# Linear-attention kv blocks: sixteen 128-column matmuls replaced by pairs on 64-column tiles, placed ahead of the normalizer's batch

## The chip, the cores and the metric

The kernel runs on one core of one Trainium2 chip. The metric is the device time of one execution in microseconds (us), lower is better. Each run lists the span and clock of one core alone, so there is no other to compare with, and a run counts as fast when it is within 1.5% of the fastest of its kernel.

## The reference

Two branches are mixed by a gate. Only branch A matters here: linear attention with 32 heads of 16 columns.

```python
qkv = (x @ wqkv)...            # x: (1, 2048, 512); H = 32 heads of Dh = 16
pq, pk = phi(q), phi(k)        # phi(t) = where(t > 0, t + 1, exp(t)) + 1e-6
kv  = einsum("bhsd,bhse->bhde", pk, v)     # one 16 x 16 block per head
z   = einsum("bhsd->bhd", pk)
num = einsum("bhqd,bhde->bhqe", pq, kv)
den = einsum("bhqd,bhd->bhq", pq, z) + 1e-6
a   = (num / den) @ wo
# ... branch B: layer norm, two matmuls over the sequence (w1, w2) with a gelu between
out = g * a + (1 - g) * b
```

## The kernel before

The kernel never forms v. It accumulates gT = (pk transposed times x) transposed, and gets the kv blocks from gT and the weights wv. Only the 16 x 16 blocks on the diagonal are wanted, so the product is taken for four diagonal blocks of 128 x 128 and multiplied with a mask. The masked blocks times wo give W2, which is used by the output tiles.

```python
    def kv_matmuls():                              # ND = 4, P = 128
        kvps = bank("kvps")                        # 128 x 512 f32
        for j in range(ND):
            for k in range(ND):
                mm(
                    kvps[:, j * P : (j + 1) * P], wv_sb[:, k, j * P : (j + 1) * P],
                    gT[:, k, j * P : (j + 1) * P], k == 0, k == ND - 1,
                )
        nc.vector.tensor_tensor(
            out=kvbdT[:], in0=kvps[:].rearrange("p (j d) -> p j d", j=ND),
            in1=mask[:].unsqueeze(1).to_broadcast([P, ND, P]), op=ALU.mult,
        )

    def den_matmuls():                             # the normalizer: already on four 32-column tiles
        denps = bank("denps")
        for j in range(ND):
            for c in range(NSC):                   # NSC = 4
                mm(
                    denps[32 * c : 32 * c + 32, :], Z32[:, 32 * j : 32 * j + 32], pqT[:, j, c * SC : (c + 1) * SC],
                    j == 0, j == ND - 1, tile_position=(0, 32 * c),
                )
        ...  # rden = reciprocal(denps) on VectorE

    for t in range(NT):                            # the q-projection stage, NT = 16
        for jj in range(NB0):
            mm(accs[jj][:], w1c[0][:, t, jj * P : (jj + 1) * P], hs[:, t, :], t == 0, t == NT - 1)
        q_block(t)
        ...
        if t == 4:
            kv_matmuls()
        ...
    for j in range(NB0, NF):                       # the w1 blocks, sixteen matmuls each
        ...  # acc += w1 block j times hs; gelu(j, acc)
        if j == NB0 + 2:
            z_matmuls()
        if j == NB0 + 3:
            den_matmuls()
            gate_sums()
            ...
        if NB0 + 4 <= j < NB0 + 4 + ND:
            w2_matmul(j - NB0 - 4)                 # W2 = masked kv blocks times wo
    ...  # the output tiles: aps (A branch) and yps (B branch), 16 of them
```

## Time and profile before

| | before |
|---|---|
| time, median of 3 runs | 165.60 us (165.58 to 165.94) |
| span of the profiled execution | 163.6 us |
| tensor engine busy | 159.9 us, 98% |
| chain of waits | 98% tensor engine |
| kv batch on the chain | 0.89 us |

The first view is the page: the busy time of each engine with its share of the span and its number of instructions, and the chain of waits by engine.

```profile
PE 159.9 (98%) x785; PEld 73.6 (45%) x785; DVE 87.8 (54%) x200; ACT 58.7 (36%) x90; POOL 18.3 (11%) x37
...
PE 98%; DVE 0%; issue 0%
```

The chain is 98% tensor engine, so every nanosecond of its stream counts, and nothing else does as long as it stays hidden. The second view is the same chain in order of time. Its columns are the start in us, the length in us, what ran and how many of it.

```profile
40.07 0.86 PE qacc L108 x4
40.93 0.89 PE kvps L108 x16
41.82 0.65 PE uacc L108 x3
...
68.99 3.47 PE uacc L108 x16
72.46 0.98 PE denps L108 x16
73.44 3.56 PE uacc L108 x16
```

The kv batch is 0.89 us, sixteen steps of 56 ns. A 512-column matmul takes a step of 216 ns, so sixteen of them take 3.45 us; the normalizer's sixteen take only 0.98 us, because four tiles work at once (their starts lie within 10 ns, below). The block behind it takes 3.56 instead of 3.45 us. The timeline shows why. Its columns are start, length, engine, line, operation, output and inputs, sizes, count, and in brackets the idle time before it. PE is a matmul and PEld a weight load. A recorded matmul is longer than its step (379 ns on the page for 512 columns, against 216 ns from start to start), so the records overlap, and steps are read from starts.

```profile
40.55 1.09 PEld L108 LDWEIGHTS <-wv_sb 128*128 128x128 bf16 x16
40.77 1.06 PE L108 MATMUL kvps<-gT,wv_sb 128*128 128x128 bf16 x16
41.61 0.37 PEld L108 LDWEIGHTS <-w1c 128*128 128x128 bf16 x3
41.66 0.81 PE L108 MATMUL uacc<-hs,w1c 128*128 128x512 bf16 x3
...
72.39 0.55 PEld L108 LDWEIGHTS <-Z 128*32 128x32 bf16 x16 [0.42 <-issue]
72.39 1.05 PE L108 MATMUL denps<-pqT,Z 128*32 128x512 bf16 x16
...
73.36 3.14 PEld L108 LDWEIGHTS <-w1c 128*128 128x128 bf16 x16 [0.42 <-issue]
73.37 3.63 PE L108 MATMUL uacc<-hs,w1c 128*128 128x512 bf16 x16
```

Around the kv batch the weight loads run ahead of the matmuls (40.55 against 40.77 us) without a pause. Around the normalizer they pause, "0.42 <-issue", both when the 32-column tiles begin and when the full array returns. In the trace's records the last full matmul starts at 72.079 us and the first normalizer matmul at 72.388, 309 ns later, and the last normalizer matmul starts at 73.056 and the next full one at 73.368, 312 ns later. The step would be 216 ns in both places, so by these starts a change of tiling costs 93 to 96 ns. The sixteen normalizer matmuls start in four groups, the four tiles of a group within 10 ns.

### The profile page before, as it was taken

How to read it: one execution, taken by the hardware profiler on the slowest of the kernel's cores; microseconds unless marked ns; L12 is line 12 of the kernel's file. 1: busy time of each engine (PE TensorE's matmuls, PEld its weight loads, DVE VectorE, ACT ScalarE, POOL GpSimd, SP SyncE). 2: the span in 40 equal slices, each digit the busy share in tenths (PEclk: the TensorE clock that was granted, in tenths of full speed). 3: DMA queues.
4: the chain of work that ended last, by engine and by line, in shares of the span. 5: the costliest groups of instructions: out<-in, count | busy, mean ns of one | idle time of the engine just before them, and what ended most of it. 6: DMA issues, size and time to landing. Idle time of an engine off the chain costs nothing.

```text
span 163.6 us, 2078 instructions
## 1 busy us (share of the span) xinstructions
PE 159.9 (98%) x785; PEld 73.6 (45%) x785; DVE 87.8 (54%) x200; ACT 58.7 (36%) x90; POOL 18.3 (11%) x37
## 2 busy tenths in 40 slices
PE   7999999999999999999999999999999999999993
PEld 3444444444544444434444444444444444444452
DVE  0599999958999999109995301156221111111112
ACT  3463386658478373311332113111112222211110
POOL 5000710200200000001055500050000000000000
DMA  5999999999930005800993499932010000111001
GB/s 152 242 243 236 294 300 344 349 348 348 317 78 0 0 0 188 264 0 0 277 303 109 149 289 307 337 126 98 32 36 32 32 32 32 42 50 41 32 32 32
DMA packets 30057, 25.05 MB, mean 153 GB/s; under 512 B 7968, under 2 KB 29472, under 8 KB 30048
## 3 DMA queue, kind: packets, MB, share of 16 engines
q1 hardware_dynamic: 28032, 22.02, 45.5%
q0 software_dynamic: 1440, 2.38, 5.4%
q10 hardware_dynamic: 576, 0.52, 1.1%
q8 instruction: 6, 0.10, 0.2%
q14 instruction: 3, 0.02, 0.0%
HBM read 21.11 MB, written 2.23 MB: 143 GB/s over the span
## 4 chain that ended last, share of the span: by engine, by line
PE 98%; DVE 0%; issue 0%
PE uacc L108 30%; PE yps L108 30%; PE kacc L108 9%; PE aps L108 8%; PE qacc L108 8%; PE gacc L108 8%; PE wps L108 2%; PE pt L194 1%; PE denps L108 1%; PE kvps L108 1%; DVE ot L474 0%; PE zps L108 0%; PE pt L323 0%
## 5 line engine op out<-in xcount | busy, mean ns | idle before, releaser
L108 PE MATMUL uacc<-hs,w1c 128*128 128x512 bf16 x224 | 52.1, 379 | 0.0
L108 PE MATMUL yps<-uT,w2c 128*128 128x512 bf16 (+2 forms) x238 | 51.0, 366 | 0.0
L474 DVE SCALAR_TENSOR_TENSOR ot<-yps,c,a_sc 128x512 bf16<-128x512 f32 (+2 forms) x17 | 12.2, 720 | 45.9 <-PE yps L108 45.8
L108 PEld LDWEIGHTS <-w2c 128*128 128x128 bf16 x238 | 22.8, 98 | 25.9
L108 PEld LDWEIGHTS <-w1c 128*128 128x128 bf16 x224 | 21.7, 98 | 26.0 <-issue 0.4
L461 ACT ACTIVATE a_sc<-aps,c,gg 128x512 f32<-128x512 f32 x16 | 12.4, 778 | 46.7 <-PE aps L108 43.0
L317 ACT ACTIVATE uT<-uacc,bcol 128x512 bf16<-128x512 f32 x14 | 9.3, 687 | 27.7 <-PE uacc L108 27.7
L108 PE MATMUL aps<-W2sb,pqT 128*128 128x512 bf16 x64 | 16.4, 379 | 0.0
L108 PE MATMUL qacc<-xT,wq_sb 128*128 128x512 bf16 x64 | 16.4, 379 | 0.0
L108 PE MATMUL kacc<-wk_sb,xT 128*128 128x512 bf16 x64 | 16.4, 385 | 0.0
L108 PE MATMUL gacc<-pk,xs 128*128 128x512 bf16 x64 | 15.8, 379 | 0.0
L244 ACT ACTIVATE hs<-xs,nmr,rstd 128x512 bf16<-128x512 bf16 x16 | 12.8, 805 | 1.9 <-DVE nmr L238 1.9
L204 ACT ACTIVATE e<-qacc 128x512 bf16<-128x512 f32 x16 | 9.6, 597 | 10.1 <-PE qacc L108 9.2
L413 POOL DMA_DIRECT2D rex<-rd_dram x16 | 9.5, 603 | 23.0 <-DVE pqT L415 18.2
L204 ACT ACTIVATE e<-kacc 128x512 bf16<-128x512 f32 x16 | 9.3, 595 | 6.9 <-PE kacc L108 6.8
L208 DVE SCALAR_TENSOR_TENSOR pk<-kacc,e 128x512 bf16<-128x512 f32 x16 | 11.1, 692 | 0.6
L208 DVE SCALAR_TENSOR_TENSOR pqT<-qacc,e 128x512 bf16<-128x512 f32 x16 | 11.1, 692 | 0.6
L228 DVE BATCH_NORM_STATS2 stats<-xs 128x6 f32<-128x512 bf16 x16 | 10.9, 682 | 0.0
L205 DVE TENSOR_SCALAR e<-e 128x512 bf16<-128x512 bf16 x32 | 9.0, 282 | 3.3 <-ACT e L204 3.3
L400 DVE CUSTOM_DVE_ANT_0 junk<-xs,gw_b 128x512 bf16<-128x512 bf16 x16 | 9.8, 685 | 0.0
L269 DVE TENSOR_TENSOR zacc<-zacc,pk 128x512 f32<-128x512 f32 x14 | 9.6, 686 | 0.2
L108 PEld LDWEIGHTS <-wq_sb 128*128 128x128 bf16 x64 | 6.3, 98 | 7.5
(64 smaller groups left out, 70.1 us busy)
## 6 DMA issues: line engine op xcount, KB each, us to landing
w2c<-in_B_w_dram SPq DMA_DIRECT2D x8, 896.0 KB, 7.5
w1c<-in_B_w_dram SPq DMA_DIRECT2D x2, 2048.0 KB, 15.5
w1c<-in_B_w_dram SPq DMA_DIRECT2D x3, 1024.0 KB, 12.3
rex<-rd_dram POOLq DMA_DIRECT2D x16, 128.0 KB, 2.9
out_dram<-ot SPq DMA_DIRECT2D x15, 128.0 KB, 1.7
xs<-in_A_x_dram SPq DMA_DIRECT2D x3, 512.0 KB, 4.5
wq_sb<-in_A_wqkv_dram SPq DMA_DIRECT2D x1, 512.0 KB, 6.8
wv_sb<-in_A_wqkv_dram SPq DMA_DIRECT2D x1, 512.0 KB, 12.3
```

The costliest lines, as they stand in the source:

```text
L108: nc.tensor.matmul(o, lhsT=lhsT, rhs=rhs, start=start, stop=stop, **kw)
L204: nc.scalar.activation(out=e[:], in_=acc[:], func=ACT.Exp)
L205: nc.vector.tensor_scalar(out=e[:], in0=e[:], scalar1=1.0, scalar2=PHI_EPS, op0=ALU.min, op1=ALU.add)
L208: nc.vector.scalar_tensor_tensor(out=dst, in0=acc[:], scalar=0.0, in1=e[:], op0=ALU.max, op1=ALU.add)
L228: nc.vector.bn_stats(out=stats[:], in_=xs[:, t, :])
L244: nc.scalar.activation(out=hs[:, t, :], in_=xs[:, t, :], func=ACT.Identity, scale=rstd[:, t : t + 1], bias=nmr[:, t : t + 1],)
L269: nc.vector.tensor_tensor(out=zacc[:], in0=first, in1=pk[:, t, :], op=ALU.add)
L317: nc.scalar.activation(out=uT[:, j, :], in_=acc[:], func=ACT.Gelu_apprx_tanh, bias=bcol[:, j : j + 1])
L400: nc.vector.tensor_tensor_reduce(out=junk[:], in0=xs[:, t, :], in1=gw_b[:], scale=1.0, scalar=0.0, op0=ALU.mult, op1=ALU.add, accum_out=gp ...
L413: nc.gpsimd.dma_start(out=rex[:], in_=src.unsqueeze(1).to_broadcast([8, HEAD, SC]))
L461: nc.scalar.activation(out=a_sc[:], in_=aps[:], func=ACT.Identity, scale=gg[:, t : t + 1], bias=c2[:, t : t + 1],)
L474: nc.vector.scalar_tensor_tensor(out=ot[:, :W], in0=yps[:, :W], scalar=c1[:, t : t + 1], in1=a_sc[:, cs], op0=ALU.mult, op1=ALU.add,)
```

## The change

The intent is to compute only the two 64 x 64 diagonal blocks of each 128 x 128 block, on two 64-column tiles of the array that are to work side by side, as the normalizer's four do (starts within 10 ns), and to put them where the array is in a column-tiled mode anyway. The masking becomes two half-size operations, the untouched half of kvbdT is cleared once at the start, and the W2 products come one w1 block later.

```diff
+    nc.vector.memset(kvbdT[:], 0.0)
...
+    H2 = P // 2
     def kv_matmuls():
         kvps = bank("kvps")
         for j in range(ND):
             for k in range(ND):
-                mm(
-                    kvps[:, j * P : (j + 1) * P], wv_sb[:, k, j * P : (j + 1) * P],
-                    gT[:, k, j * P : (j + 1) * P], k == 0, k == ND - 1,
-                )
-        nc.vector.tensor_tensor(out=kvbdT[:], ... whole bank times mask ...)
+                for h in (0, H2):
+                    c = slice(j * P + h, j * P + h + H2)
+                    mm(
+                        kvps[h : h + H2, c], wv_sb[:, k, c], gT[:, k, c], k == 0, k == ND - 1,
+                        tile_position=(0, h),
+                    )
+        for h in (0, H2):
+            d = slice(h, h + H2)
+            nc.vector.tensor_tensor(out=kvbdT[d, :, d], ... the half of the bank times mask[d, d] ...)
...
-        if t == 4:
-            kv_matmuls()
...
         if j == NB0 + 3:
+            kv_matmuls()
             den_matmuls()
...
-        if NB0 + 4 <= j < NB0 + 4 + ND:
-            w2_matmul(j - NB0 - 4)
+        if NB0 + 5 <= j < NB0 + 5 + ND:
+            w2_matmul(j - NB0 - 5)
```

More of the change, by code (lines that the diff above doesn't have):

```diff
@@ L329, in kv_matmuls @@
             for k in range(ND):
-                mm(
-                    kvps[:, j * P : (j + 1) * P], wv_sb[:, k, j * P : (j + 1) * P],
-                    gT[:, k, j * P : (j + 1) * P], k == 0, k == ND - 1,
-                )
-        nc.vector.tensor_tensor(
-            out=kvbdT[:], in0=kvps[:].rearrange("p (j d) -> p j d", j=ND),
-            in1=mask[:].unsqueeze(1).to_broadcast([P, ND, P]), op=ALU.mult,
-        )
+                for h in (0, H2):
[6 more added lines that the diff above has]
+            d = slice(h, h + H2)
+            nc.vector.tensor_tensor(
+                out=kvbdT[d, :, d],
+                in0=kvps[d, :].rearrange("p (j d) -> p j d", j=ND)[:, :, d],
+                in1=mask[d, d].unsqueeze(1).to_broadcast([H2, ND, H2]), op=ALU.mult,
+            )
     def z_split():
```

## The prediction

> **What bounds the kernel.** The tensor engine. The page's first part has it busy 98% of a 163.6 us span, and the chain of waits is 98% matmuls, end to end: the pieces in order of time show no gap beyond about 0.1 us after the start. The granted clock is 1.00. So only what the change does to the tensor engine's own stream counts, unless it makes a new wait.
>
> **What the change removes.** The chain's pieces give the sixteen full-width kv matmuls 0.89 us at 40.93 us. In the timeline they start 56 ns apart, and the stream before and after runs at its usual 216 ns per 512 columns. All 0.89 us lie on the critical path. VectorE loses one 128x512 masking multiply (0.68 us) in a stretch where it is busy 12.8 of 13.2 us, but no matmul there waits for it, so that is worth nothing.
>
> **What it adds.** 32 matmuls 64 columns wide on two column tiles, directly ahead of the normalizer's batch. That batch shows how column tiles behave here: its sixteen 512-column matmuls start in groups of four (72.39, 72.61, 72.83, 73.05 us), four tiles within about 10 ns, so tiles do run side by side. It also shows what entering and leaving costs: the last full-array matmul starts at 72.08 us and the first normalizer matmul 0.31 us later, the last group at 73.05 us and the next full-array matmul 0.32 us later; both should be 0.22. So about 0.1 us per switch. [...] The new order is full, 64, 32, full: three switches for two, so the sharing of a stage saves no switch and adds one of about 0.1 us (64 to 32).
>
> The 32 matmuls make sixteen pairs. Streaming 64 columns takes half of 56 ns, about 28 ns per pair, 0.45 us in all (estimate). But each tile needs new weights for every matmul. [...] no trace shows yet what a 64-column load then costs, because the normalizer hides its loads behind 216 ns of streaming. [...] My central value is 0.75 us.
>
> Sum: -0.89 + 0.75 + 0.1 = about 0. [...]
>
> **What moves off the path.** The kv blocks' masking (two 64-partition multiplies, about 0.4 us each by the width of the old one) run beside the normalizer matmuls, so the reciprocal hardly moves. The W2 products come one w1 block (3.45 us) later and still end before their first use at 98 us. VectorE idles 7.2 us before the gate's tanh, so the normalizer's scaling keeps slack. The new zero fill falls into VectorE's 3.0 us wait at the start. The built program's order shows the kv and normalizer matmuls waiting only for accumulator evictions some 10 us old.
>
> **Predicted time: 165.6 us, 165.2 to 166.3.** Faster by over 2%: 0.5%; within 2%: 99%; slower: 0.5%.
>
> **What would show it right.** q-projection phase about 0.9 us shorter; from the last full-array matmul before kv to the first normalizer matmul about 0.8 to 1.1 us; gaps of about 0.1 us at three switches; the chain still 98% tensor engine; the w1 blocks and the last phase unchanged.
>
> **What would make it wrong.** 64-column loads that serialise; [...] matmuls of a pair that don't overlap; a wait of the W2 products or of the first output tile on VectorE.

The prediction is printed with cuts. Its sum came to about 0: 0.89 us go, 0.75 us for the batch and 0.1 us for the switch come. Of the 0.75 us only the 0.45 us of streaming is worked out from the trace; the term for the weight loads, and with it the slow end of the range, rested on nothing that a trace or run shows. The fast end of the range, given as -0.35 us, is streaming alone: -0.89 + 0.45 + 0.1. At a change of tiling the trace shows a gap of 93 to 96 ns and not what happens in it.

## The result, and the profile after

| | before | after |
|---|---|---|
| time, median of 6 runs each | 165.78 us (165.58 to 165.94) | 165.56 us (165.02 to 165.72) |
| ratio | | 0.9983, 95% interval 0.9967 to 0.9999 |
| from the first matmul of the q-projection stage to the last of the kernel | 127.396 us | 127.126 us |
| kv batch, from its first start to the next batch's first start | 0.893 us | 0.625 us |

A ratio is the mean time of one kernel's fast runs over that of the other's fast runs of the same rounds, so it is not quite the ratio of the medians. By the clock: 0.17% with an interval that just misses 1.

The third row is the sharper measure. It is the difference of two start times in the trace (for before, 33.158 and 160.554 us). What lies ahead of it, the loading of the first tiles, ends between 33.05 and 33.70 us in the thirteen fast profiles, with no pattern by kernel that I could see, and this alone blurs the whole time by a few tenths of a us. Behind the normalizer the stream repeats to a nanosecond: from the last normalizer start to the last matmul of the kernel it took 87.498 or 87.499 us in every profile of before, after and the first eight experiments. The stretch is 0.270 us shorter after the change; 0.22 us is the difference of the medians.

The page of the changed kernel:

```profile
PE 158.7 (97%) x787; PEld 73.3 (45%) x801; DVE 88.3 (54%) x202; ACT 58.7 (36%) x90; POOL 18.3 (11%) x37
...
PE 95%; DMA 2%; issue 1%; ACT 0%; DVE 0%
```

Two traps lie here. There are 801 weight loads but only 787 matmuls: the trace lost 14 records. Each lost one shows as a step of 432 in place of 216 ns, and as "issue" in the chain; the stretch above is unchanged by them, which is the proof that they are no stalls. The 2% of DMA is the wait for the first tiles of x at the start, which has nothing to do with the change. The chain in order of time, and the timeline (columns as before):

```profile
68.18 3.47 PE uacc L108 x16
71.65 0.62 PE kvps L108 x32
72.28 0.98 PE denps L108 x16
```

```profile
71.58 0.58 PEld L108 LDWEIGHTS <-wv_sb 128*64 128x64 bf16 x32 [0.42 <-issue]
71.58 0.69 PE L108 MATMUL kvps<-gT,wv_sb 128*64 128x64 bf16 x32
...
72.20 0.55 PEld L108 LDWEIGHTS <-Z 128*32 128x32 bf16 x16
72.20 1.05 PE L108 MATMUL denps<-pqT,Z 128*32 128x512 bf16 x16
72.32 0.86 DVE L341 TENSOR_TENSOR kvbdT<-kvps,mask 64x256 bf16<-64x256 f32 x2 [3.91 <-PE kvps L108]
73.18 4.86 PEld L108 LDWEIGHTS <-w1c 128*128 128x128 bf16 x24 [0.42 <-issue]
...
73.31 3.36 DVE L379 RECIPROCAL rden<-denps 128x512 bf16<-128x512 f32 x1
```

The pairs start 31.7 ns apart (the first 52), both tiles of a pair within 4 ns, so 32 matmuls take 0.499 us from first to last start. The first normalizer matmul follows 126 ns behind the last kv matmul: one step of 32 and a change of tiling of 94 ns. The entry (309 ns) and the exit (312 ns) are those of the normalizer alone before. The sum is exact: 0.893 us of the old batch go, 0.499 + 0.126 come, 0.893 - 0.625 = 0.268 us.

Off the path nothing woke up. The masking (two times 0.42 us) ends before the reciprocal can start. VectorE's spare time ahead of the output stage, shown by its wait for the gate's tanh in the view of who waited for whom (total us, times, longest), shrank from this in the kernel before

```profile
DVE gg L447 <- ACT gth L446: 7.2, 1, 7.2
```

to this in the changed one,

```profile
DVE gg L454 <- ACT gth L453: 6.3, 1, 6.3
```

and is still there.

### The profile page after: what moved, and what is told of

It reads as the page before. It is cut to its first block, busy times and chain, and to the rows that moved or that the text cites. A ratio compares the mean times of both kernels' runs of the same rounds, so it can differ in the third digit from the quotient of the medians.

```text
span 163.4 us, 2099 instructions
## 1 busy us (share of the span) xinstructions
PE 158.7 (97%) x787; PEld 73.3 (45%) x801; DVE 88.3 (54%) x202; ACT 58.7 (36%) x90; POOL 18.3 (11%) x37
## 4 chain that ended last, share of the span: by engine, by line
PE 95%; DMA 2%; issue 1%; ACT 0%; DVE 0%
PE uacc L108 30%; PE yps L108 29%; PE aps L108 9%; PE gacc L108 8%; PE qacc L108 8%; PE kacc L108 8%; DMA xs<-in_A_x_dram 2%; PE pt L195 1%; PE denps L108 1%; PE wps L108 1%; PE kvps L108 0%; ACT xT L199 0%; DVE ot L481 0%; PE zps L108 0%; PE pt L324 0%
## 5 line engine op out<-in xcount | busy, mean ns | idle before, releaser
L108 PEld LDWEIGHTS <-pqT 128*128 128x128 bf16 x64 | 6.3, 98 | 7.6
```

Of the source, the lines that this page charges most:

```text
L108: nc.tensor.matmul(o, lhsT=lhsT, rhs=rhs, start=start, stop=stop, **kw)
```

## Experiments

The theory after the result: the gain is the pace of the pairs (32 ns for two against 56 ns for one) less one change of tiling; the place itself is worth nothing except for the changes of tiling it saves; weight loads of the two tiles don't limit (this last part stayed open). Rivals: the gain comes from leaving the q-projection stage, where VectorE is full (busy 12.82 of the 13.20 us from 41.8 to 55 us in the kernel before); the 0.1 us ahead of the normalizer is no cost of changing the tiling; the narrower matmuls, and not the tiles side by side, set the pace. "Stretch" is the q-projection stage's first matmul to the kernel's last, as in the table above; it is read from one profile of each kernel. The rounds ran on several chips, each with its own runs of before, so ratios compare runs of one chip, and stretches also cross chips.

| run | ratio to before (95% interval) | stretch, us | against before |
|---|---|---|---|
| before | 1 | 127.396 | |
| the change | 0.9983 (0.9967 to 0.9999) | 127.126 | -0.270 |
| e1_move_only | 1.0011 (0.9997 to 1.0026) | 127.396 | 0.000 |
| e2_pairs_in_place | 0.9981 (0.9966 to 0.9996) | 127.236 | -0.160 |
| e3_quads | 0.9973 (0.9956 to 0.9989) | 126.997 | -0.399 |
| e8_tile_by_tile | 0.9977 (0.9963 to 0.9992) | 127.152 | -0.244 |
| e9_quads_interleaved | 0.9970 (0.9957 to 0.9984) | 126.894 | -0.502 |
| e11_sixteen_then_sixteen | 1.0011 (0.9997 to 1.0025) | 127.530 | +0.134 |
| e4_pairs_x9 | 1.0297 (1.0279 to 1.0314) | 132.107 | +4.711 |
| e5_full_x9 | 1.0426 (1.0409 to 1.0444) | 134.542 | +7.146 |
| e6_grouped | 1.0602 (1.0575 to 1.0629) | 137.539 | +10.143 |
| e7_alternated | 1.0662 (1.0638 to 1.0686) | 138.344 | +10.948 |
| e12_far_apart_again | 1.0191 (1.0178 to 1.0204) | 130.570 | +3.174 |

Every experiment's kernel computed the right result.

### Only the place: e1_move_only

```diff
 # the kernel before, its sixteen full-width kv matmuls and one masking kept
-        if t == 4:
-            kv_matmuls()
         if j == NB0 + 3:
+            kv_matmuls()
             den_matmuls()
 # and the W2 products one block later, as in the change
```

> The sixteen full-width kv matmuls of the kernel before, moved to the new place ahead of the normalizer's batch, with their one full-width masking; no column tiles for kv. Theory (the gain is the tiles' own streaming, half the columns per step): the move is worth nothing, ratio to before 1.000 within 0.001; kv starts 56 ns apart, 0.89 us[...]. Rival (the gain comes from taking kv out of the q-projection stage, where VectorE is full and evictions could hold accumulators): ratio 0.998, as the whole change.

The stretch is 127.396 us, the same as before to the nanosecond. The chain in order of time:

```profile
72.04 0.89 PE kvps L108 x16
72.93 0.98 PE denps L108 x16
```

The move alone is worth nothing, and the rival that looked to VectorE falls. The whole time read 1.0011 here and not 1.000, because this kernel's stretch began late (33.635 us, before 33.158); the interval holds 1.

### Only the tiles: e2_pairs_in_place

```diff
 # the changed kernel, but
         if j == NB0 + 3:
-            kv_matmuls()
             den_matmuls()
+        if t == 4:
+            kv_matmuls()        # back in the q-projection stage; W2 products back at NB0 + 4
```

> The paired 64-column tiles, left at the old place in the q-projection stage. Theory: pairs 32 ns apart, 0.51 us, plus two switches of 0.1 us of its own: 0.71 against 0.89 us, so 0.18 us less than before (ratio 0.999) and 0.1 us more than the changed kernel, because the normalizer's batch needs its own two switches as well (four in all against three). Rival (a switch costs nothing by itself, the gaps belong to the normalizer's first weight loads): no gap at the kv batch, 0.38 us less than before, ratio 0.9977.

The stretch is 0.160 us shorter than before, against 0.18 expected, and 0.110 longer than the changed kernel's. The chain in order of time:

```profile
39.96 0.86 PE qacc L108 x4
40.82 0.63 PE kvps L108 x32
41.45 0.16 issue
41.61 0.59 PE uacc L108 x2
```

The entry costs 310 ns from start to start where 216 is the step. The "issue" of 0.16 us is no stall: of the three w1 matmuls here only two are in the trace. Two weight loads for them stand at 41.376 and 41.391 us but the first recorded matmul at 41.607, 355 ns behind the last kv matmul. Less the step of 216 of the lost one, that leaves an exit of 139 ns, and with it the sum gives the 0.160 us of the stretch. So pairs in the old place pay two changes of tiling of their own, and the new place saves one of them. The sharing of the stage is worth 0.11 us, and only compared with pairs elsewhere.

### Nine batches: e4_pairs_x9 and e5_full_x9

```diff
-        for j in range(ND):
+        for j in [j for _ in range(9) for j in range(ND)]:     # in the changed kernel, and in e1_move_only
```

> The changed kernel with its kv batch issued nine times over (each overwrites the same result), to size one batch in the whole time. Theory: 8 more batches of 16 pairs at 31.7 ns, 4.06 us more than the changed kernel. Rival (the trace's starts hide a cost that is paid elsewhere): more than 4.6 us.

> The same nine-fold repetition of the full-width batch at the same place. Theory: 8 more batches of 16 matmuls at 55.8 ns, 7.1 us more than before; so one batch of full width costs 0.39 us more than one of pairs. Rival (a full-width batch's cost is partly hidden): less than 6.5 us.

Eight more full-width batches cost 7.146 us, 0.893 each, as read from one. Eight more batches of pairs cost 132.107 - 127.126 = 4.981 us where 4.06 was expected; by the number alone this is the rival's case, more than 4.6. By the records the steps from pair to pair are 31 or 32 ns, the first 52; but at 76.45 us the stream stops once. The chain in order of time:

```profile
72.02 4.42 PE kvps L108 x272
76.45 0.74 issue
77.18 0.44 PE kvps L108 x16
```

One step from pair to pair takes 936 ns. Without this pause the eight batches cost 4.981 - 0.936 + 0.032 = 4.08 us, 0.51 each. The page's row of the instruction queue went from 6 packets to 8, and the trace has two fetches of 16 KB, at 71.31 and 74.88 us, which took 0.92 and 0.96 us, just ahead of the pause; in the kernel before these fetches lie 23 to 28 us apart. The grouped run below pauses too, and in both the pause stands behind the same number of short matmuls, 272, with as many weight loads. Whether the pause is a wait for instructions was not shown, for no run took that cause away. A single batch, which is what the change has, does not meet it: no step in the changed kernel's stretch is over 442 ns, and that one holds a lost record.

### The price of changing the tiling: e6_grouped and e7_alternated

```diff
-            kv_matmuls()
-            den_matmuls()
+            for b in "KKKKKKKKDDDDDDDD":       # e6_grouped; "KDKDKDKDKDKDKDKD" in e7_alternated
+                kv_mm(kvps) if b == "K" else den_mm(denps)
+            kv_evict(kvps)
+            den_evict(denps)
```

> Eight kv batches of pairs, then eight normalizer batches (results overwritten with the same values): three switches. Theory: 7 x 0.507 + 7 x 0.86 = 9.6 us more than the changed kernel.

> The same eight and eight batches, but alternating, kv, normalizer, kv and so on: fourteen more changes between 64-column and 32-column tiles than grouped. Theory ([...]about 0.10 us both ways): 14 x 0.10 = 1.4 us more than the grouped one, ratio between the two about 1.008. Rival (the 0.1 us at the first normalizer matmul is a one-time cost, a first load or a wait for its data, and not the switch): no difference.

The grouped run took 10.413 us more in the stretch than the changed kernel, where 9.6 was expected. By the medians the alternating order costs 176.73 - 175.80 = 0.93 us more, 0.80 by the stretch, where 1.4 was expected. The grouped run has a pause like that of the nine batches (one step of 1026 ns in place of 216, at 76.8 us), and the alternating run has none. Without these 0.81 us the grouped run costs 9.60, as expected, and fourteen changes cost 0.805 + 0.81 = 1.61 us, 0.115 us each. The alternating trace shows it directly and without correction; its chain begins:

```profile
71.69 0.62 PE kvps L108 x32
72.31 0.98 PE denps L108 x16
73.29 0.63 PE kvps L108 x32
73.91 0.98 PE denps L108 x16
```

From one kv batch to the next takes 1602 ns, where sixteen pair steps and four group steps make 507 + 863 = 1370; half of the difference is 0.116 us. Of it 94 ns is the gap, and most of the rest the slower first step after the gap (52 in place of 32 ns for kv, 226 in place of 216 for the normalizer). The change between two column tilings costs as much as that to and from the full array (a gap of 94 ns against 96 and 93), and the rival, a one-time cost, falls.

### Four tiles: e3_quads

```diff
-    H2 = P // 2
+    H2 = P // 4                                 # 64 matmuls of 32 columns, the normalizer's own tiling
...
-                for h in (0, H2):
+                for h in range(0, P, H2):       # and the masking in four parts
```

> 64 kv matmuls of 32 columns on four column tiles, the same tiling as the normalizer's batch, at the new place. Theory (streaming sets the pace[...]): the switch between kv and the normalizer goes (0.10 us saved), and the group of four starts every 16 to 25 ns: 16 groups, 0.26 to 0.40 us against 0.51. In all 0.2 to 0.35 us less than the changed kernel, ratio to before about 0.9965. Rival (issue of the instructions sets the pace, about 1.7 ns per record in this trace but two records per matmul, or some 25 ns per weight load and tile): 64 loads in a row cost 0.5 us or more, and only the switch is saved.

The chain in order of time:

```profile
68.64 3.47 PE uacc L108 x16
72.11 0.59 PE kvps L108 x64
72.70 0.88 PE denps L108 x16
```

The first normalizer matmul starts 8 ns behind the last kv matmul: with the same tiling on both sides there is no gap like the 94 ns. The stretch is 0.129 us shorter than the changed kernel's, almost all of it the change of tiling saved, where 0.2 to 0.35 was expected. So the part of my theory about the pace missed: the batch itself took 0.478 us from first to last start against 0.499, not 0.26 to 0.40, and the rival (some 0.5 us, only the switch saved) came nearer. Its first eight groups start 25 ns apart, the later ones 34, in even steps of 8 to 9 ns per matmul.

### Filling in behind the normalizer: e9_quads_interleaved

```diff
-            kv_matmuls()
-            den_matmuls()
+            for b in range(ND):
+                den_mm(denps, b)                # four matmuls, 216 ns of streaming
+                kv_mm(kvps, b)                  # sixteen, on the same four tiles
+            den_evict(denps)
+            kv_evict(kvps)
```

> Four 32-column tiles for kv as in the quads run, but each block's sixteen kv matmuls stand behind four normalizer matmuls (216 ns of streaming) in place of all 64 in a row. In the quads run the first eight groups of four started about 25 ns apart and the later ones about 34 ns apart with even steps of 8 to 9 ns. Theory (the later ones wait for the issue of two instructions per matmul at about 4.2 ns each, the first ones stood in the queue already): with the queue refilled behind each normalizer group all sixteen groups take about 25 ns, 0.40 us in place of 0.48, so 0.06 to 0.10 us less than the quads run in the trace, from the first q-projection-stage matmul to the last one of the kernel 126.9 us; too small for the whole time, which should be 0.997 of before. Rival (the later pace is that of loading weights): 34 ns for half of the groups again, nothing gained.

All sixteen groups now start 25 ns apart, and the stretch is 126.894 us, as expected 126.9. The chain in order of time, with two of the four rounds:

```profile
71.80 0.33 PE denps L108 x4
72.12 0.09 PE kvps L108 x16
72.22 0.23 PE denps L108 x4
72.44 0.09 PE kvps L108 x16
```

So a new weight set with every matmul does not by itself force 34 ns per group: the even 8 to 9 ns per matmul of the quads run appear when 64 short matmuls stand in a row, and go when sixteen at a time stand behind long ones. That the issue of instructions is the limit of the long row, as the theory had it, fits but was not tested apart. By the stretch this is the best version found, 0.50 us less than before; by the clock, 0.9970, it cannot be told from the changed kernel.

### Does the order of the tiles matter: e8_tile_by_tile, e10_tiles_far_apart, e12_far_apart_again, e11_sixteen_then_sixteen

```diff
 # changed kernel:                 for j: for k: for h     left, right, left, right, ...
 # e8_tile_by_tile:                for j: for h: for k     four left, four right, ...
 # e11_sixteen_then_sixteen:       for h: for j: for k     sixteen left, sixteen right
 # e10, e12:                       for h: four times (for j: for k)     64 left, 64 right
```

> The changed kernel with the order of its 32 matmuls changed: for each block the four of one tile and then the four of the other, in place of alternating. Theory (the two tiles run side by side only when neighbours in the stream use different tiles): each matmul waits for the one before on its tile, about 30 ns each, 0.95 us for the batch against 0.51, so 0.4 us more than the changed kernel and a ratio to before of about 1.001. Rival (the queue finds the parallel work by itself, or the pair's gain is only the narrower matmul): 0.51 us as before.

My theory of this run missed. The batch took 0.523 us against 0.499, as the rival expected. The chain in order of time:

```profile
71.55 0.65 PE kvps L108 x32
72.20 0.98 PE denps L108 x16
```

The starts are at 0, 13, 52, 66, 84, 97, 116 and 129 ns, two interleaved rows with the pace of one tile. So either matmuls of the right tile overtake waiting ones of the left, or 16 ns is the pace of a 64-column matmul on any tile. The next runs separate these.

> The 64-column tiles, but the sixteen matmuls of one tile issued four times over, 64 in a row, and then the 64 of the other tile (results overwritten with the same values). Theory A (a tile takes a new matmul every 32 ns; the queue lets the other tile's matmuls overtake, but only as far as it is deep): 64 alone at 32 ns, less what the queue can reach, so 2.6 to 4.1 us for the 128. Theory B (the pace is 16 ns per 64-column matmul, whichever tile it is on, and side by side is not the reason): even steps of 16 ns and 2.05 us for the 128.

> The far-apart kernel again, because its profile fell in a slow state (clock 0.565). Expected in the fast state: each tile's 64 matmuls 32 ns apart with even steps, 16 ns steps only for a short stretch where the second tile begins, 3.8 to 4.0 us for the 128, ratio to before about 1.020.

> The changed kernel with all sixteen matmuls of the left tile first and then all sixteen of the right one; the same 32 matmuls. Theory (one tile takes a matmul every 32 ns, and a matmul of the other tile may overtake only a few places): only the middle overlaps; in the slow profile of the far-apart run some six of one tile ran beside six of the other, so 26 steps of 32 ns, 0.83 us for the batch in place of 0.51, and 0.3 us more than the changed kernel in the trace (127.4 us from the first q-projection-stage matmul to the last one of the kernel). Rival (the queue sees the whole batch, 64 instructions): 0.52 us, 127.15 us.

The profile of e10 fell into an execution of 290.22 us at a clock of 0.565, so only its three fast times are used (168.83 to 169.17 us, ratio 1.0192), and e12 is the same kernel again. In e12 the starts are 31 or 32 ns apart for the first sixty matmuls of the left tile and again for the right tile's from the sixty-ninth on, in all 3.94 us from first to last start. Its chain in order of time:

```profile
71.69 4.07 PE kvps L108 x128
75.75 0.98 PE denps L108 x16
```

Only for eight matmuls around the border do two rows interleave. By these starts one tile takes a matmul every 31 or 32 ns, theory A, and a few matmuls of one tile began beside a few of the other that stand ahead of them in the program, four of each if the eight are shared evenly. In e11 the batch took 0.902 us from first to last start, again with eight starts interleaved in the middle. Its chain in order of time:

```profile
68.35 3.47 PE uacc L108 x16
71.83 1.03 PE kvps L108 x32
72.86 0.98 PE denps L108 x16
```

The stretch is 0.404 us longer than the changed kernel's, more than the 0.3 expected, and 0.134 longer than before: with the tiles one after the other the change would have been a loss. The reach seen is those four or so, which is just what tile by tile needs. The records don't name the tile, so which matmul a start belongs to is inferred from the pace.

## Why the prediction was right

The predicted time was 165.6 us, 165.2 to 166.3, and 165.56 was measured. That the two agree to 0.04 us is luck. The prediction's sum was about no change to a kernel that had read 165.60 us; in the rounds of the result that kernel read 165.78, and the change took 0.22 us off it by the clock and 0.27 by the stretch. The range was right, and the measured change lies near its fast end, which the prediction gave to streaming alone.

- **The bound.** Right. The chain stayed on the tensor engine and the whole difference is found in its stream, 0.270 us of it between two start times, 0.268 us by the sum of its parts. The check "still 98% tensor engine" was not met by the page, which reads 95%; the difference is the wait for x at the start and the lost records, and no wait came up inside the stretch.
- **What goes: 0.89 us.** Right, 0.893 us, and exactly that again in eight repetitions (7.146 / 8).
- **Three changes of tiling for two, 0.1 us each.** Right. The step from 64 to 32 columns has a gap of 94 ns, and 0.115 us with its slower first steps when repeated. With four tiles it is gone, 8 ns.
- **"My central value is 0.75 us" for the 32 matmuls.** This term was mis-sized. It is 0.53 us: sixteen pairs at 31.7 ns, and a first step that is 20 ns longer. The prediction let the weight loads decide, with a figure that no trace showed. By the starts a tile took a new weight set and a matmul every 31 or 32 ns, for sixty matmuls in a row in e12, and working the second tile beside it added nothing to that step, for the pairs start 31.7 ns apart too. The size is close to the 28 ns that the prediction estimated for streaming alone, from the 56 ns of a full-width matmul. In the kernel before, the eight full-array matmuls of zps, each with 128 columns of new weights and 8 streamed columns, start 25 to 29 ns apart. Whether streaming or the load sets the 31.7 ns stays open, because every run that narrowed the kv weights narrowed the streamed columns with them. The net was therefore -0.27 us and not about 0. The prediction's own check, 0.8 to 1.1 us from the last full matmul to the first normalizer matmul, did hold (72.205 - 71.271 = 0.934 us), but with 0.75 us for the batch it would have read 0.22 + 0.09 + 0.75 + 0.1 = 1.16: check and central value did not fit each other.
- **What moves off the path.** Right. The reciprocal starts at 73.31 instead of 73.49 us, and VectorE still waits 6.3 us ahead of the gate. The move alone changed the stretch by nothing.
- **"q-projection phase about 0.9 us shorter."** Right. The kv batch is gone from it: the last full matmul ahead of the normalizer stage starts 0.81 us earlier (71.271 against 72.079) although the stage began 0.09 us later.

## What to carry to other kernels

Where a matmul batch is on the critical path, size a change of it by start-to-start steps and by the gaps at its ends, and sum them; here this gave the gain to 2 ns, while run times could barely tell it from nothing. In these runs small column tiles paid twice. They paid by working side by side: the same 32 matmuls took 0.499 us when the stream changed tiles with every matmul, 0.523 with every four, and 0.902 with sixteen and sixteen; nothing between four and sixteen was run. And they paid by sharing one tiling with the batch beside them, since each change of tiling left a gap of about 0.1 us (93 to 96 ns in before and in the changed kernel): four tiles next to the normalizer's four had none (8 ns), while two tiles next door saved only one change of two, 0.110 us. The 32-column matmuls did best between long ones of the same tiling, sixteen behind every four of the normalizer's: the stretch was 0.103 us shorter than with all 64 in a row. Try these in another kernel, and measure the steps there.
